# Routing attention and a bilinear feed-forward on one core: who sums the exponentials of the first batch element, and when weights are rounded

## The chip, the cores and the metric

The kernel runs on one core of a Trainium2 chip. The metric is device time in microseconds (us), and less is better. TensorE (PE) multiplies matrices into PSUM, VectorE (DVE), ScalarE (ACT) and GpSimd (POOL) work element by element, and SyncE (SP) issues most of the transfers. Each engine takes its instructions in the order in which the program gives them.

## What is computed

The input has 4 batch elements, 8 heads, 768 rows and a head dimension of 64. Queries and keys are assigned to one of 16 centroids per head, and a query sees only the keys of its own centroid. The attention output of each row (8 heads by 64) is the input of a feed-forward that multiplies two projections with each other.

```python
q_assign = np.argmax(np.einsum('bhsd,hcd->bhsc', q_n, c_n), axis=-1)
k_assign = np.argmax(np.einsum('bhsd,hcd->bhsc', k_n, c_n), axis=-1)
mask = q_assign[:, :, :, None] == k_assign[:, :, None, :]
scores = np.where(mask, scale * np.matmul(q, k.transpose(0, 1, 3, 2)), -1e9)
attn = np.exp(scores - np.max(scores, axis=-1, keepdims=True))
attn = attn / (np.sum(attn, axis=-1, keepdims=True) + 1e-09)
x = np.matmul(attn, v)            # then (B, H, S, D) -> (B*S, H*D)
out = (x @ w_a) * (x @ w_b) @ w_out    # w_a, w_b: 512 x 1536, w_out: 1536 x 512
```

The weights come as 64-bit numbers and are rounded to 32 bits on the chip.

## The kernel before

**The units.** Two heads form a pair, and there are 16 pairs, four (HP) to a batch element. The 768 query columns of a pair are two halves of 384 (HB), and its keys are six tiles of 128 (NJ). A unit u is one pair p, one half hf and one key tile j. The main loop (L580) runs over groups g of two units, six groups to a pair; l is g mod 6, so a half ends after l = 2 and after l = 5. The four pairs of the first batch element are the groups 0 to 23.

**A group.** `score` (L403) multiplies keys with queries for both units, the masking product of the one-hots first, and ScalarE exponentiates into a tile pt, of which there are four. For the two units of the group before, `add_up` (L431) adds each pt into acc, and `weigh` (L448) multiplies with the values into O. In the first batch element a half has ten additions of 128 x 384: two of them, for the second head at j = 1 and j = 3, are GpSimd's, and eight are VectorE's. In the later batch elements GpSimd has seven of ten. Then comes a preparation step of the next pair (`prep_steps`, L376): transposes at l = 0, similarity to the centroids at l = 1, the choice of a centroid by five VectorE instructions at l = 2 (`prep_assign`, L339), and at l = 4 both transposes of the one-hots (`prep_onehot`, L358).

**Denominators.** When a half has been summed, `denominators` (L465) multiplies acc with ones on TensorE, so that each column's sum stands in all rows, and ScalarE copies it to den. This happens at l = 4 and at l = 1, one group after the last addition was issued. `normalize` (L478) takes the reciprocal in three VectorE instructions at the end of a group (l = 5 and l = 3) and multiplies xT by it on GpSimd. `check_inverses` (L488) then reads den on ScalarE in the next group, right behind the two exponentials.

**The weights.** There are 36 parts of 128 x 512, 24 of w_a and w_b in three thirds of their columns, then 12 of w_out. `round_w` (L243) costs VectorE four instructions, ScalarE one (`size`) and GpSimd one addition, and `flush_w` (L270) ends it with a fifth VectorE instruction, issued in the next group or ahead of the next part. `size` has one buffer, so that ScalarE's `size` of a part waits for the flush of the part before. `due` (L564) says in which group each part is rounded. Behind each part `load_w` issues the transfer of the part after the next on SyncE's queue.

**The feed-forward.** When all four pairs of a half have been normalised, `ffn_ready` (L542) queues the pieces of that block. A piece is one projection of 128 output columns, and a group takes as many pieces as its share of columns (`PER_GROUP`) allows, about three. For the first batch element the first eight pieces use the first third of w_a and w_b alone. All of `ps_m`, the PSUM pool of the transposes, the denominators and the pieces, has three buffers.

**Names.** `ps_s` is the PSUM pool of the scores (two buffers), `ps_m` that of the rest (three), `ptp` the pool of pt (four), `wtp` that of the rounding's scratch tiles.

Of the kernel before, what the change touches and what calls it, by code (L numbers as in the profile page):

```python
# [30 lines left out]
P = 128  # L31
# [3 lines left out]
@with_exitstack  # L35
def kernel(
    ctx: ExitStack,
    tc: tile.TileContext,
    q: bass.AP,
    k: bass.AP,  # L40
    v: bass.AP,
    centroids: bass.AP,
    moe_w_a: bass.AP,
    moe_w_b: bass.AP,
    moe_w_out: bass.AP,
    out: bass.AP,
):
    nc = tc.nc

    B, H, S, D = q.shape  # L50
    NC = centroids.shape[1]
    DM, DF = moe_w_a.shape
    NJ = S // P
    HP = H // 2
    NCH = DM // P
    NF = DF // P
    assert D == 64 and NC == 16 and NJ == 6 and DM == H * D and H * NC == P

    const = ctx.enter_context(tc.tile_pool(name="const", bufs=1))
    ctx.enter_context(tc.manual_schedule())  # L60


    csb = const.tile([P, D], FP32)
    nc.scalar.dma_start(out=csb, in_=centroids.rearrange("h c d -> (h c) d"))
    c = {
        "wa_sb": const.tile([P, NCH, DF], FP32, name="wa_sb"),
        "wb_sb": const.tile([P, NCH, DF], FP32, name="wb_sb"),
        "wo_sb": const.tile([P, NF, DM], FP32, name="wo_sb"),
    }

    one = const.tile([P, 1], FP32)
    nc.vector.memset(one, 1.0)
    ce = const.tile([P, 1], FP32)
    ident = c["ident"] = const.tile([P, P], FP32, name="ident")
    masks.make_identity(nc, ident)
    identb = c["identb"] = const.tile([P, P], BF16, name="identb")
    ones = c["ones"] = const.tile([P, D], FP32, name="ones")
    nc.vector.memset(ones, 1.0)

    rank_i = const.tile([P, NC], INT32)  # L80
    nc.gpsimd.iota(rank_i, pattern=[[-1, NC]], base=NC, channel_multiplier=0)
    rank = c["rank"] = const.tile([P, NC], FP32, name="rank")

    cn = const.tile([P, 2, D], FP32)

    def centroids_in():

        nc.scalar.activation(out=ce, in_=one, func=AF.Sqrt)
        csq = const.tile([P, D], FP32)
        cs2 = const.tile([P, 1], FP32)  # L90
        nc.vector.tensor_tensor(out=csq, in0=csb, in1=csb, op=ALU.mult)
        nc.vector.tensor_reduce(out=cs2, in_=csq, axis=AX.X, op=ALU.add)
        cn0 = const.tile([P, 1], FP32)
        nc.scalar.activation(out=cn0, in_=cs2, func=AF.Sqrt)

        nc.scalar.activation(out=ce, in_=cn0, func=AF.Exp)

        cnm = const.tile([P, 1], FP32)
        nc.vector.tensor_scalar(out=cnm, in0=cn0, scalar1=1e-30, scalar2=None,
                                op0=ALU.max)  # L100
        cnr = const.tile([P, 1], FP32)
        nc.vector.reciprocal(out=cnr, in_=cnm)
        cnt = const.tile([P, 1], FP32)
        nc.vector.scalar_tensor_tensor(out=cnt, in0=cs2, scalar=cnr[:, 0:1],
                                       in1=cn0, op0=ALU.mult, op1=ALU.add)
        cne = const.tile([P, 1], FP32)
        nc.vector.tensor_scalar(out=cne, in0=cnt, scalar1=0.5, scalar2=1e-6,
                                op0=ALU.mult, op1=ALU.add)
        crinv = const.tile([P, 1], FP32)
        nc.vector.reciprocal(out=crinv, in_=cne)  # L110
        for a in range(2):
            nc.vector.tensor_scalar(out=cn[:, a, :], in0=csb,
                                    scalar1=crinv[:, 0:1], scalar2=None,
                                    op0=ALU.mult)
        nc.vector.tensor_copy(out=rank, in_=rank_i)
        nc.vector.tensor_copy(out=identb, in_=ident)

    cT = c["cT"] = const.tile([P, P], FP32, name="cT")  # L120
    cTb = c["cTb"] = const.tile([P, HP, 2 * NC], FP32, name="cTb")
    nc.gpsimd.memset(cTb, 0.0)

    n_far = const.tile([1, 1], INT32, name="n_far")
    with ExitStack() as fast:
        short_path(nc, tc, fast, c, cn, centroids_in, n_far, q, k, v, moe_w_a, moe_w_b,
                   moe_w_out, out)

    redo = nc.values_load(n_far[0:1, 0:1], min_val=0, max_val=P,
                          skip_runtime_bounds_check_because="a count of rows")  # L130
    with tc.If(redo > 0):
        with ExitStack() as slow:
            long_path(nc, tc, slow, c, q, k, v, out)


def short_path(nc, tc, ctx, c, cn, centroids_in, n_far, q, k, v, moe_w_a,
               moe_w_b, moe_w_out, out):


    B, H, S, D = q.shape  # L140
# [23 lines left out]
    xtp = pool("xtp", 2)  # L164
    hp_ = pool("hp", 2)
    hap = pool("hap", 2)
    yp = pool("yp", 1)
    rawp = pool("rawp", 2)
    wtp = pool("wtp", 1)
    ps_s = pool("ps_s", 2, PS)  # L170
    ps_m = pool("ps_m", 3, PS)
    ps_o = pool("ps_o", 1, PS)
# [70 lines left out]
    def round_w(i):  # L243
        flush_w()
        w = w_parts[i][0]
        wi = w.bitcast(INT32)
        raw = raws.pop(i)
        halves = lambda dt: raw.bitcast(dt).rearrange("p (n two) -> p n two", two=2)
        lo, hi = halves(UINT32)[:, :, 0], halves(INT32)[:, :, 1]


        nc.vector.tensor_scalar(out=wi, in0=hi, scalar1=3, scalar2=0x3FFFFFF8,
                                op0=ALU.logical_shift_left,
                                op1=ALU.bitwise_and)
        nc.vector.scalar_tensor_tensor(out=wi, in0=hi, scalar=SIGN_TOP, in1=wi,
                                       op0=ALU.bitwise_and, op1=ALU.bitwise_or)

        rest = wtp.tile([P, WN], FP32, name="rest")
        nc.vector.tensor_scalar(out=rest.bitcast(INT32), in0=wi,
                                scalar1=SIGN_EXP, scalar2=None,  # L260
                                op0=ALU.bitwise_and)
        nc.vector.scalar_tensor_tensor(out=rest, in0=lo, scalar=2.0 ** -52,  # L262
                                       in1=rest, op0=ALU.mult, op1=ALU.mult)

        size = wtp.tile([P, WN], FP32, name="size")
        nc.scalar.activation(out=size, in_=halves(FP32)[:, :, 1], func=AF.Abs)  # L266
        nc.gpsimd.tensor_tensor(out=w, in0=w, in1=rest, op=ALU.add)
        flush.append((w, size))
# [107 lines left out]
    def prep_steps(p):  # L376
# [3 lines left out]
        def both(*fs):  # L380
# [4 lines left out]
            both(lambda: prep_sim(p), lambda: load_v(p)),  # L385
            lambda: prep_assign(prep_across(p)),
            lambda: None,
            both(lambda: prep_onehot(p, 0), lambda: prep_onehot(p, 1)),
            lambda: None,
        ]  # L390

# [38 lines left out]

    def add_up(u):  # L431
        p, hf, j = where(u)
        if j == 0:
            return
        if j == 1:
            accs[p, hf] = accp.tile([P, 2, HB], FP32, name="acc")
        acc = accs[p, hf]
        for a in range(2):
            if p < HP:
                eng = nc.gpsimd if a == 1 and j in (1, 3) else nc.vector  # L440
            else:
                eng = nc.gpsimd if a == 1 or j in (2, 4) else nc.vector
            eng.tensor_tensor(  # L443
                out=acc[:, a, :],
                in0=probs[u - 1][:, a, :] if j == 1 else acc[:, a, :],
                in1=probs[u][:, a, :], op=ALU.add)
# [17 lines left out]

    def denominators(p, hf):  # L465

        ps = ps_m.tile([P, 512], FP32, name="m")
        acc = accs.pop((p, hf))
        for a in range(2):
            nc.tensor.matmul(out=ps[a * D:(a + 1) * D, 0:HB], lhsT=ones,  # L470
                             rhs=acc[:, a, :], start=True, stop=True)
        den = denp.tile([P, HB], FP32, name="den")
        n = 4 * p + 2 * hf
        nc.scalar.activation(out=den, in_=ps[:, 0:HB], func=AF.Copy,  # L474
# [22 lines left out]
    def ffn_block(b, blk):  # L497
# [25 lines left out]
        def down(n):  # L523
            ps = ps_m.tile([P, 512], FP32, name="m")
            for f in range(NF):
                nc.tensor.matmul(out=ps, lhsT=box["h"][:, f, n * P:(n + 1) * P],  # L526
                                 rhs=wo_sb[:, f, :],
                                 start=(f == 0), stop=(f == NF - 1))
            y = yp.tile([P, DM], FP32, name="y")
            nc.scalar.copy(out=y, in_=ps)  # L530
            rows = out[b * S:(b + 1) * S, :].rearrange(
                "(p j) n -> p j n", j=NJ)[:, 3 * blk + n, :]
# [24 lines left out]
    GPP = UPP // 2  # L557
    NG = NPAIR * GPP
    PER_GROUP = (2 * NF * NCH * HB + 3 * NF * DM) * 2 // (HP * GPP)
    credit = 0  # L560

    due = {g: [i] for i, g in enumerate((1, 4, 6, 7, 10, 13, 16, 19))}  # L564
    for i in range(8, len(w_parts)):
        due.setdefault(20 + int((i - 8) / 1.5), []).append(i)

    prep_transpose(0, 0)
    centroids_across()
    prep_transpose(0, 1)  # L570
    prep_transpose(0, 2)
    load_v(0)
    load_w(0)
    load_w(1)
# [5 lines left out]
    for g in range(NG + 3):  # L580
# [13 lines left out]
            weigh(before)  # L594
        if g < NG:
            ready[l]()
        if g % 3 == 1 and 3 < g:
            denominators(*divmod(g // 3 - 1, 2))
        parts = due.get(g, [])

# [17 lines left out]
        if l == 0 and p + 1 < NPAIR:  # L618
            prep_transpose(p + 1, 2)
            load(p + 2)  # L620
        if l == 5 or l == 3 and 6 < g < NG or g == NG + 2:
            ph = (p, 0) if l == 5 else (p - 1, 1)
            normalize(*ph)
            if ph[0] % HP == HP - 1:
                ffn_ready(ph[0] // HP, ph[1])
# [248 lines left out]
```

## Time and profile before

| | us |
|---|---|
| median of 3 runs | 1214.0 (1213.69 to 1214.56) |
| the profiled execution | 1212.46 |
| its span, first to last instruction | 1210.6 |
| TensorE busy in it | 1154.6 (95%) |
| VectorE, ScalarE, GpSimd busy | 408.1, 333.2, 276.6 |

The page divides the span into 40 equal slices. TensorE's busy digits are 6987597999 in the first ten slices and 9 in nearly all later ones; VectorE's are 5999967566 in the first ten. A busy digit of TensorE says that matmuls were in flight, not that they ran at the full clock: the row PEclk gives the granted clock beside it.

### The profile page before, as it was taken

Reading aid. Unit: us, or ns where it says so; the run is one execution under the profiler, and the core shown is the slowest. Engines: PE = TensorE matmul, PEld = TensorE weight load, DVE = VectorE, ACT = ScalarE, POOL = GpSimd, SP = SyncE. Lnnn points to the kernel's source line nnn. Section 1 sums busy time; section 2 is a strip of 40 time slices with the busy share of each in tenths; the row PEclk is TensorE's granted clock in tenths of the full one; section 3 lists DMA queues with packets and bytes.
Section 4 is the critical chain, followed back from the end, with each engine's and each line's share of the span. In section 5 each row is a group of like instructions: output and inputs, shape, how many; then the busy total and the mean of one; then the engine's idle time right before and its main releaser. Section 6 shows DMA issues by size and latency. Waiting matters only on the chain.

```text
span 1210.6 us, 11842 instructions
## 1 busy us (share of the span) xinstructions
PE 1154.6 (95%) x4723; PEld 578.0 (48%) x4723; DVE 408.1 (34%) x614; ACT 333.2 (28%) x608; POOL 276.6 (23%) x261
## 2 busy tenths in 40 slices
PE   6987597999999999999999999999999999999998
PEld 3433253555554445554455544555445544554553
DVE  5999967566621211222022221222111220200100
ACT  4654333323323222322322222321322211100000
POOL 2333324334413221222221132121211321000000
PEclk9999798999999999999999999999999999999999
DMA  5323332321202001010200101010000000000000
GB/s 155 94 75 84 95 92 87 88 74 53 74 1 57 18 22 35 1 40 9 57 1 1 39 18 48 1 40 1 18 22 1 1 9 18 1 1 26 1 1 28
DMA packets 60782, 44.91 MB, mean 37 GB/s; under 512 B 48432, under 2 KB 53040, under 8 KB 60720
## 3 DMA queue, kind: packets, MB, share of 16 engines
q1 hardware_dynamic: 59744, 42.21, 12.1%
q10 hardware_dynamic: 976, 1.87, 0.4%
q8 instruction: 39, 0.64, 0.2%
q14 instruction: 23, 0.19, 0.1%
HBM read 37.78 MB, written 6.29 MB: 36 GB/s over the span
## 4 chain that ended last, share of the span: by engine, by line
PE 86%; DVE 8%; issue 2%; POOL 2%; ACT 2%; DMA 0%; DVEq 0%; POOLq 0%; ACTq 0%
PE m L505 42%; PE m L526 21%; PE O L454 8%; PE s L420 8%; DVE den L483 3%; PE s L411 3%; PE m L307 2%; PE m L470 1%; DVE acc L443 1%; PE m L323 1%; POOL xT L485 1%; DVE wa_sb L274 1%; DVE rest L262 1%; PE m L334 1%; DVE wb_sb L274 0%
## 5 line engine op out<-in xcount | busy, mean ns | idle before, releaser
L505 PE MATMUL m<-xT,wa_sb 128*128 128x384 f32 x768 | 268.6, 493 | 16.7 <-ACT ohT L374 13.4
L505 PE MATMUL m<-xT,wb_sb 128*128 128x384 f32 x768 | 268.3, 493 | 0.0
L526 PE MATMUL m<-wo_sb,h 128*128 128x512 f32 x576 | 251.2, 594 | 0.0
L520 DVE TENSOR_TENSOR h<-ha,m 128x384 f32<-128x384 f32 x96 | 53.1, 554 | 536.2 <-PE m L505 536.1
L443 POOL TENSOR_TENSOR acc<-acc,pt 128x384 f32<-128x384 f32 x152 | 155.4, 1035 | 241.6 <-ACT pt L427 233.9
L505 PEld LDWEIGHTS m<-xT,wa_sb 128*128 128x128 f32 x768 | 145.1, 192 | 120.6 <-ACT ohT L374 18.0
L505 PEld LDWEIGHTS m<-xT,wb_sb 128*128 128x128 f32 x768 | 145.4, 192 | 111.3 <-ACT pt L427 10.2
L427 ACT ACTIVATE pt<-s 128x768 f32<-128x768 f32 x192 | 145.7, 809 | 124.8 <-PE s L420 89.0
L526 PEld LDWEIGHTS m<-wo_sb,h 128*128 128x128 f32 x576 | 108.7, 191 | 133.9 <-issue 129.7
L454 PE MATMUL O<-pt,v 128*64 128x384 f32 x768 | 145.0, 499 | 0.7 <-ACT xT L462 0.7
L420 PE MATMUL s<-qkT 64*128 64x384 f32 x768 | 144.4, 496 | 0.0
L516 ACT COPY ha<-m 128x384 f32<-128x384 f32 x96 | 45.9, 478 | 351.5 <-PE m L505 351.5
L443 DVE TENSOR_TENSOR acc<-acc,pt 128x384 f32<-128x384 f32 x104 | 87.1, 868 | 140.0 <-POOL acc L443 140.0
L485 POOL TENSOR_TENSOR xT<-xT,den 128x384 f32<-128x384 f32 x32 | 34.8, 1088 | 344.7 <-DVE den L483 343.1
L454 PEld LDWEIGHTS O<-pt,v 128*64 128x64 f32 x768 | 46.8, 136 | 88.5 <-issue 84.8
L420 PEld LDWEIGHTS s<-qkT 64*128 64x128 f32 x768 | 73.2, 193 | 32.1 <-issue 2.4
L530 ACT COPY y<-m 128x512 f32<-128x512 f32 x24 | 14.0, 585 | 255.4 <-PE m L526 195.6
L483 DVE RECIPROCAL den<-den 128x128 f32<-128x128 f32 x96 | 82.2, 912 | 5.5 <-ACT den L474 5.5
L411 PE MATMUL s<-ohT 64*128 64x384 bf16 x384 | 50.3, 334 | 22.9 <-ACT pt L427 22.2
L411 PEld LDWEIGHTS <-ohT 64*128 64x128 bf16 x384 | 12.2, 94 | 73.3 <-issue 63.0
L443 POOL TENSOR_TENSOR acc<-pt 128x384 f32<-128x384 f32 x32 | 37.7, 1179 | 36.5 <-ACT pt L427 36.5
L266 ACT ACTIVATE size<-raw 128x512 f32<-128x512 f32 x36 | 24.6, 685 | 51.2 <-DVE wa_sb L274 19.7
(82 smaller groups left out, 516.1 us busy)
## 6 DMA issues: line engine op xcount, KB each, us to landing
raw<-in_moe_w_out_dram SPq DMA_DIRECT2D x12, 512.0 KB, 3.2
out_dram<-y SPq DMA_DIRECT2D x24, 256.0 KB, 2.0
qk<-in_q_dram SPq DMA_DIRECT2D x30, 192.0 KB, 3.9
qk<-in_k_dram SPq DMA_DIRECT2D x30, 192.0 KB, 4.2
v<-in_v_dram SPq DMA_DIRECT2D x15, 384.0 KB, 4.6
raw<-in_moe_w_a_dram SPq DMA_DIRECT2D x11, 512.0 KB, 3.5
raw<-in_moe_w_b_dram SPq DMA_DIRECT2D x11, 512.0 KB, 3.5
raw<-in_moe_w_a_dram ACTq DMA_DIRECT2D x1, 512.0 KB, 4.5
```

Source lines behind the costliest of these rows:

```text
L266: nc.scalar.activation(out=size, in_=halves(FP32)[:, :, 1], func=AF.Abs)
L411: nc.tensor.matmul(out=s[:, a, 0:HB], lhsT=ohTs[p][r, S + j * P:S + (j + 1) * P], rhs=ohTs[p][r, hf * HB:(hf + 1) * HB], start=True, stop= ...
L420: nc.tensor.matmul(out=s[:, a, 0:HB], lhsT=qkTs[p][r, S + j * P:S + (j + 1) * P], rhs=qkTs[p][r, hf * HB:(hf + 1) * HB], start=False, stop ...
L427: nc.scalar.activation(out=pt, in_=s[:, :, 0:HB], func=AF.Exp, scale=SCALE)
L443: eng.tensor_tensor(out=acc[:, a, :], in0=probs[u - 1][:, a, :] if j == 1 else acc[:, a, :], in1=probs[u][:, a, :], op=ALU.add)
L454: nc.tensor.matmul(out=O_of[0][a * D:(a + 1) * D, 0:HB], lhsT=vs[p][:, a, j, :], rhs=probs[u][:, a, :], start=(j == 0), stop=(j == NJ - 1))
L483: nc.vector.reciprocal(out=part, in_=part)
L485: nc.gpsimd.tensor_tensor(out=x, in0=x, in1=den, op=ALU.mult)
L505: nc.tensor.matmul(out=ps[:, 0:HB], lhsT=w_sb[:, ch, f * P:(f + 1) * P], rhs=xTs[b][:, ch, t0:t0 + HB], start=(ch == 0), stop=(ch == NCH - 1))
L516: nc.scalar.copy(out=box["a"], in_=ps[:, 0:HB])
L520: nc.vector.tensor_tensor(out=box["h"][:, f, :], in0=box["a"], in1=ps[:, 0:HB], op=ALU.mult)
L526: nc.tensor.matmul(out=ps, lhsT=box["h"][:, f, n * P:(n + 1) * P], rhs=wo_sb[:, f, :], start=(f == 0), stop=(f == NF - 1))
```

## The change

It touches five things.

1. In the first batch element the last key tile of a half (j = 5) is no longer added on VectorE. `denominators` multiplies its pt with ones as well, into the same PSUM sums, with two more matmuls.
2. The remaining additions of the first batch element, eight per half, are all on VectorE; GpSimd has none of them there.
3. `denominators` runs one group earlier in the first batch element (l = 3 and l = 0, in the group in which the last addition is issued), and `normalize` at the end of l = 4 and l = 1.
4. Parts are rounded at g = 0, 3, 6, ... 21, so that eight parts, a third of w_a and w_b, precede group 23 (before, 14 parts were due by the end of group 23); the other 28 follow from group 23, 1.75 a group instead of 1.5 from group 20. `size` gets two buffers, and the output tile y takes the buffer of `rest`.
5. `prep_onehot` of the queries moves from the preparation step of l = 4 to the end of that group, and two small casts of the start are issued later.

```diff
+    def casts():
+        nc.vector.tensor_copy(out=rank, in_=rank_i)
+        nc.vector.tensor_copy(out=identb, in_=ident)
...
-    yp = pool("yp", 1)
+    sizep = pool("sizep", 2)
...
-        size = wtp.tile([P, WN], FP32, name="size")
+        size = sizep.tile([P, WN], FP32, name="size")
...
-            both(lambda: prep_onehot(p, 0), lambda: prep_onehot(p, 1)),
+            lambda: prep_onehot(p, 1),
...
-        if j == 0:
+        if j == 0 or j == NJ - 1 and p < HP:
             return
...
-            if p < HP:
-                eng = nc.gpsimd if a == 1 and j in (1, 3) else nc.vector
-            else:
-                eng = nc.gpsimd if a == 1 or j in (2, 4) else nc.vector
+            many = p >= HP and (a == 1 or j in (2, 4))
+            eng = nc.gpsimd if many else nc.vector
...
-        acc = accs.pop((p, hf))
-        for a in range(2):
-            nc.tensor.matmul(out=ps[a * D:(a + 1) * D, 0:HB], lhsT=ones,
-                             rhs=acc[:, a, :], start=True, stop=True)
+        terms = [accs.pop((p, hf))]
+        if p < HP:
+            terms.append(probs[p * UPP + hf * NJ + NJ - 1])
+        for n, t in enumerate(terms):
+            for a in range(2):
+                nc.tensor.matmul(out=ps[a * D:(a + 1) * D, 0:HB], lhsT=ones,
+                                 rhs=t[:, a, :], start=(n == 0),
+                                 stop=(n == len(terms) - 1))
...
-            y = yp.tile([P, DM], FP32, name="y")
+            y = wtp.tile([P, DM], FP32, name="rest")
...
+    EARLY = HP * GPP + 1
...
-    due = {g: [i] for i, g in enumerate((1, 4, 6, 7, 10, 13, 16, 19))}
+    due = {3 * i: [i] for i in range(8)}
     for i in range(8, len(w_parts)):
-        due.setdefault(20 + int((i - 8) / 1.5), []).append(i)
+        due.setdefault(23 + int((i - 8) / 1.75), []).append(i)
...
+    casts()
...
-        if g % 3 == 1 and 3 < g:
+        late = int(g > EARLY)
+        if g % 3 == late and 0 < g - late:
             denominators(*divmod(g // 3 - 1, 2))
...
-        if l == 5 or l == 3 and 6 < g < NG or g == NG + 2:
-            ph = (p, 0) if l == 5 else (p - 1, 1)
+        if l == 4 and p + 1 < NPAIR:
+            prep_onehot(p + 1, 0)
+        if g <= EARLY:
+            first, second = 4, 1
+        else:
+            first, second = 5, 3 if g < NG else 2
+        ph = {first: (p, 0), second: (p - 1, 1)}.get(l)
+        if ph in den_of:
             normalize(*ph)
```

## Rows read from the trace of the kernel before

**Rows 1.** Six stretches: length; busy PE, PEld, DVE, ACT, POOL; clock; DMA; GB/s.

```profile
17.10:40.35 23.25, 23.22 (x152) 10.77 (x153) 18.13 (x27) 14.81 (x23) 7.10 (x6) 0.94 0.36 89
40.35:66.90 26.55, 25.24 (x165) 11.30 (x163) 25.05 (x36) 12.77 (x23) 8.29 (x8) 1.00 0.36 102
66.90:96.85 29.95, 25.99 (x165) 11.70 (x164) 29.50 (x41) 18.78 (x36) 10.97 (x9) 0.94 0.28 75
96.85:131.90 35.05, 25.90 (x163) 11.59 (x163) 33.13 (x49) 15.63 (x29) 12.19 (x10) 0.90 0.38 109
131.90:209.36 77.46, 58.57 (x233) 29.35 (x232) 56.93 (x84) 26.81 (x50) 31.34 (x27) 0.85 0.31 90
209.36:340.00 130.64, 129.58 (x555) 68.86 (x554) 78.97 (x116) 43.67 (x79) 46.48 (x42) 1.00 0.22 67
```

**Rows 2.** TensorE's waits from 17 to 132 us: total, times, longest.

```profile
PE s L411 <- ACT pt L427: 13.6, 8, 6.4
```

**Rows 3.** The same view from 132 to 210 us.

```profile
PE s L411 <- ACT pt L427: 8.6, 4, 7.6
PE m L505 <- ACT ohT L374: 7.0, 1, 7.0
PE m L505 <- POOL xT L485: 3.3, 1, 3.3
```

**Rows 4.** Timeline around group 22: start, length, what, idle before and releaser.

```profile
120.15 0.69 DVE L274 SCALAR_TENSOR_TENSOR wa_sb<-size,wa_sb 128x512 f32<-128x512 f32 x1 [1.37 <-POOL wa_sb L267]
...
120.88 0.68 ACT L266 ACTIVATE size<-raw 128x512 f32<-128x512 f32 x1 [6.48 <-DVE wa_sb L274]
...
122.30 0.51 PE L411 MATMUL s<-ohT 64*128 64x384 bf16 x2 [6.41 <-ACT pt L427]
```

**Rows 5.** Timeline, VectorE: a rounding, the reciprocals behind it, its flush.

```profile
126.56 0.41 DVE L252 TENSOR_SCALAR wa_sb<-raw 128x512 int32<-128x512 int32 x1
...
128.81 2.57 DVE L483 RECIPROCAL den<-den 128x128 f32<-128x128 f32 x3
...
131.71 1.48 DVE L274 SCALAR_TENSOR_TENSOR wa_sb<-size,wa_sb 128x512 f32<-128x512 f32 x1
```

**Rows 6.** Groups by line, 17 to 132 us: count, busy us, mean ns, idle.

```profile
L443 DVE TENSOR_TENSOR acc<-acc,pt 128x384 f32<-128x384 f32 x49 | 37.3, 818 | 0.0
L262 DVE SCALAR_TENSOR_TENSOR rest<-raw,rest 128x512 f32<-128x512 uint32 x11 | 7.7, 699 | 0.4
...
L443 POOL TENSOR_TENSOR acc<-pt 128x384 f32<-128x384 f32 x7 | 8.4, 1196 | 22.3 <-ACT pt L427 22.3
```

**Rows 7.** Timeline: additions without and with GpSimd at work beside them.

```profile
88.72 1.96 DVE L443 TENSOR_TENSOR acc<-acc,pt 128x384 f32<-128x384 f32 x4
...
97.21 2.56 DVE L443 TENSOR_TENSOR acc<-acc,pt 128x384 f32<-128x384 f32 x3
97.38 1.51 POOL L267 TENSOR_TENSOR wa_sb<-wa_sb,rest 128x512 f32<-128x512 f32 x1 [1.81 <-DVE rest L262]
```

**Rows 8.** Timeline, groups 3 and 4: TensorE's starts, VectorE's choice and additions.

```profile
29.29 0.50 PE L411 MATMUL s<-ohT 64*128 64x384 bf16 x4
29.39 0.56 DVE L343 TENSOR_REDUCE mx<-m 128x24 f32<-128x384 f32 x1 [0.67 <-PE m L334]
...
32.23 2.76 DVE L443 TENSOR_TENSOR acc<-acc,pt 128x384 f32<-128x384 f32 x4
32.45 0.50 PE L411 MATMUL s<-ohT 64*128 64x384 bf16 x4
```

**Rows 9.** Timeline, TensorE: one half's denominators, one group's products with the values.

```profile
36.38 0.87 PE L470 MATMUL m<-acc,ones 128*64 128x384 f32 x4
...
38.90 1.51 PE L454 MATMUL O<-pt,v 128*64 128x384 f32 x8
```

**Rows 10.** The chain that ended last: start, length, what (three pieces).

```profile
165.06 7.94 PE m L505 x24
```

**Rows 11.** TensorE's waits from 280 us to the end.

```profile
PE m L505 <- ACT ohT L374: 5.3, 5, 1.1
```

More of the change, by code (lines that the diff above doesn't have):

```diff
@@ L114, in centroids_in @@
                                     op0=ALU.mult)
-        nc.vector.tensor_copy(out=rank, in_=rank_i)
-        nc.vector.tensor_copy(out=identb, in_=ident)
     cT = c["cT"] = const.tile([P, P], FP32, name="cT")
@@ L125 @@
     with ExitStack() as fast:
-        short_path(nc, tc, fast, c, cn, centroids_in, n_far, q, k, v, moe_w_a, moe_w_b,
-                   moe_w_out, out)
+        short_path(nc, tc, fast, c, cn, centroids_in, casts, n_far, q, k, v,
+                   moe_w_a, moe_w_b, moe_w_out, out)
     redo = nc.values_load(n_far[0:1, 0:1], min_val=0, max_val=P,
@@ L133, with short_path @@
             long_path(nc, tc, slow, c, q, k, v, out)
-def short_path(nc, tc, ctx, c, cn, centroids_in, n_far, q, k, v, moe_w_a,
-               moe_w_b, moe_w_out, out):
+def short_path(nc, tc, ctx, c, cn, centroids_in, casts, n_far, q, k, v,
+               moe_w_a, moe_w_b, moe_w_out, out):
     B, H, S, D = q.shape
```

## The prediction

> **What bounds the kernel now.** I read the page's busy slices first: TensorE is the engine that matters, and it has holes only early. Then I cut the span where groups begin and read the busy times of each stretch [rows 1]. The first four rows are the four pairs of the first batch element. The first pair is TensorE's own speed: busy 23.22 of 23.25 us. The next three have the same work and take 26.55, 29.95 and 35.05, while VectorE's busy time climbs to 33.13 of 35.05. So from the second pair on VectorE sets the pace. The fifth row, five groups with the first feed-forward pieces, is worse: TensorE is busy 58.57 of 77.46 and its mean clock is 0.85. In the sixth row TensorE is busy 129.58 of 130.64, and from there it bounds the kernel to the end.
>
> The waits say how VectorE reaches TensorE. Up to 132 us TensorE waits 13.6 us for exponentials [rows 2], behind that 8.6 for the same, 7.0 for a copy of the one-hots and 3.3 for a normalised xT [rows 3]. The exponentials were not slow. Where two parts are rounded in one group, ScalarE stands 6.48 us at `size`, whose single buffer the flush on VectorE has not released, the exponentials of the next group are queued behind it, and TensorE stands 6.41 [rows 4].
>
> **How much there is to win.** A pair has two denominators, and the first row holds one, so a pair without stalls is 23.25 + 0.87 [rows 9] = 24.1 us. Four pairs would be 23.25 + 3 x 24.1 = 95.6; they took 131.90 - 17.10 = 114.8. Loss A: 19.2. The fifth stretch holds five groups at 24.1 / 6 = 4.0 and eleven pieces (3, 3, 2, 0 and 3 by the code's shares) at 7.94 / 3 = 2.65 [rows 10]: 20.1 + 29.1 = 49.2 of 77.46. Loss B: 28.3, of which 18.9 is idle and the rest the lower clock. Loss C: five waits of 1.06 us for the one-hots' copy, 5.3 [rows 11], and 1.06 in the sixth stretch: 6.4. Together 53.9. The last microseconds and the start stay out.
>
> **Part 1 and 2, the sums.** TensorE gets two more 128 x 64 matmuls per half (four records). Eight such records take 1.51 and four 0.87 [rows 9], so four more cost 0.64 to 0.76; I take 0.75, times eight halves 6.0 us, all on the path. The dearer end is 4 x 7.94 / 24 = 1.3 a half, 10.6, if the two heads' matmuls did not overlap as they do in these rows. VectorE still has eight additions a half: it loses two and takes over GpSimd's two. What it gains is quiet. Four additions take 1.96 alone, 0.49 each; three take 2.56 with a GpSimd addition beside them, and the mean is 0.818 [rows 6, 7]. A flush takes 0.69 alone and 1.48 beside GpSimd [rows 4, 5], so a GpSimd addition costs VectorE about 0.79. Two groups of seven GpSimd additions ran up to 132 us (1.196 us each in the one shown) [rows 6], so 14 x 0.79 = 11.1 us of VectorE goes away; the ends are 14 x 0.33 = 4.6 (one addition at the difference of the means) and 14 x 1.196 = 16.7.
>
> The Trainium skill's page "SBUF — State Buffer", section "Who interferes with whom", says that a VectorE instruction with two SBUF inputs and a GpSimd instruction that reads SBUF exclude each other for the whole instruction. By that the upper end, 16.7, would hold, and the time below would come out some 2 us shorter, as an estimate; the trace shows 1.1 us lost beside a GpSimd instruction of 1.51 [rows 7], less than that.
>
> **Part 4, the roundings.** One costs VectorE 2.25 us up to the next instruction and 0.69 to 1.48 for its flush [rows 4, 5]: 3.7 as it ran. Up to 132 us eleven ran [rows 6] of the fourteen due; eight will by the end of group 22: 3 x 3.7 = 11.1 less. VectorE's budget for the four pairs is then 105.8 (its busy times in the first four rows) - 11.1 - 11.1 + 6.0 (seven additions and a set of reciprocals that ran late, 7 x 0.49 + 2.57 [rows 5, 7]) = 89.6 us, against 95.6 + 6.0 = 101.6 for TensorE. VectorE stops being the bound there, but it is 88% loaded. The parts go to groups 23 to 28, which have eleven roundings, as many as the fifth stretch had (eight due and the three late ones), but TensorE there has 18 pieces instead of 11, so 5 x 4.0 + 4.0 + 18 x 2.65 = 72 us for six groups, against 56.93 + 7 x 0.55 (an estimate for a piece's product, like one addition beside a PSUM tile) = 61 of VectorE. The second buffer of `size` takes away the wait of rows 4 outright: ScalarE no longer stands for a flush of the part just before. SyncE's `load_w` moves with the parts, ahead of the q and k loads at l = 0; these have a whole pair to land, and I cost that at nothing. If that cover were gone, a late load would hold the transposes of the next pair by the length of a rounding, about 3 us a pair.
>
> **Part 3, the new wait.** TensorE now reaches the denominators in the group that issues the last additions (j = 4). At l = 3 these stand on VectorE behind the choice of centroids, 29.39 to 32.23 [rows 8], and take 2 x 0.49, so they end some 3.8 us after TensorE began the group; TensorE gets there 3.16 us after it (the distance of two group starts without preparation [rows 8]). That is 0.7 us a pair if VectorE is on time, and more by whatever it lags. Queued behind the denominators on TensorE are the next scores, and behind these the exponentials. At l = 0 the transposes lie ahead and cover it. I take 7 us of stalls for A in all (from 3, four times 0.7, to 15, two a half).
>
> Normalising a group or two earlier starts the first pieces in group 23 instead of 24 and the rest in 26 instead of 28, which fills TensorE where it stood. The first piece of the second block still needs the last reciprocals and a GpSimd product, some 3.8 us behind their issue; one group of scores covers most of it. I take 6 us of stalls for B (2 to 16).
>
> **Part 5.** With the queries' one-hots behind the pieces, only the keys' and the denominators' buffers of `ps_m` are held while ScalarE waits in `check_inverses`, and a piece finds the third. That should take all of C (6.4; between none and all of it). The casts are two small copies which VectorE now does while it waits for the similarities; costed at nothing, at most two additions' length, 1.0 us, if that wait were gone.
>
> **The sum.** 53.9 - 6.0 = 47.9 us at best; less 7 (A) and 6 (B): 34.9. Against the profiled execution, 1212.46 (1.9 more than its span), that is 1177.6, and the median of the runs is 1.5 above this execution: 1179.
>
> **The rivals.** *One stage keeps its loss.* For: VectorE is 88% loaded in the pairs and as a rule late, and if GpSimd's additions cost it only 4.6, its budget is 96 of 101.6; the parts of the second third are rounded one group before they are used. Against: both budgets leave room. If A keeps 18 of its 19, the time is 1190; if B keeps 20 of 28, 1193; with the dearer matmuls up to 1200.
> *Slower: the denominators wait for VectorE's lag.* The wait removed at `size` would come back as a wait for acc, at eight halves, with all of TensorE's work queued behind. It decides from 47.9 / 8 = 6.0 us a half: from there nothing is won. The longest waits of TensorE that VectorE causes now are 6.4 and 7.6 [rows 2, 3]; at 7.6 a half the time is 1214 - 47.9 + 61 = 1227. Against it: a lag of this size came from two roundings in one group, and now none has two before group 23.
> *The change does nothing.* VectorE has as many additions as before and 28 roundings crowd the start of the feed-forward: the loss moves from A to B, within 2 us of 1214.
>
> **How the numbers follow.** Forecast (1167 to 1187): 0.67. One stage keeps its loss (1187 to 1200): 0.24. Nothing: 0.04. Slower: 0.05. The range takes the first two, 1167 to 1200; its ends are the sum with least stalls (47.9 less 1) and that of the first rival. A measurement of this kernel can tell 0.2%, about 2.4 us, from no change; so faster 0.91, same 0.04, slower 0.05.
>
> **What would show it.** Right: groups 0 to 23 about 12 us shorter; no wait of ScalarE's `size` for a flush; the clock at 1.00 in nearly all of 17 to 200 us; the five later waits gone; additions near 0.5 us before the feed-forward. Wrong: TensorE waiting at the denominators for acc by more than 2 us a half, pieces waiting for w_a or w_b, or VectorE still busy over 95% in the second to fourth pair.

## The result and the profile after

The changed kernel takes 1171.4 us (median; 1170.0 to 1172.4) against 1213.9 for the kernel before: a ratio of 0.965, 95% interval 0.9633 to 0.9667, or 42.5 us less. The forecast was 1179, with a range of 1167 to 1200. The spans of the two profiled executions are 1210.6 and 1170.0 us, 40.6 us apart; what is read from traces below adds up to this figure.

All of it lies in the first 210 us and at the later transposes of the one-hots. The first fence shows the stretches of the changed kernel in the columns of [rows 1]: length; busy PE, PEld, DVE, ACT, POOL with instructions; clock; DMA share; GB/s. The first line is most of the first pair. The next three, 26 us each, are nearly pairs 2 to 4: the scores of groups 6, 12 and 18 begin at 43.64, 70.07 and 96.50, so a pair takes 26.4 us.

```profile
17.00:40.00 23.00, 21.95 (x136) 10.56 (x135) 14.96 (x27) 12.68 (x20) 2.79 (x2) 0.88 0.38 98
40.00:66.00 26.00, 25.61 (x169) 11.38 (x166) 24.09 (x37) 16.83 (x30) 5.28 (x4) 1.00 0.32 79
66.00:92.00 26.00, 25.61 (x171) 11.69 (x171) 24.08 (x37) 16.72 (x30) 5.27 (x4) 1.00 0.33 87
92.00:118.00 26.00, 25.61 (x171) 11.49 (x169) 24.09 (x38) 16.40 (x31) 5.10 (x4) 1.00 0.30 84
118.00:145.00 27.00, 27.00 (x130) 14.46 (x128) 19.98 (x33) 11.54 (x22) 7.17 (x7) 1.00 0.30 87
145.00:210.00 65.00, 64.58 (x283) 33.84 (x279) 48.10 (x71) 25.02 (x44) 27.24 (x25) 1.00 0.33 96
```

TensorE is busy 25.61 of every 26 us in the pairs and nearly all of the time behind them, with a granted clock of 1.00 from 40 us on, where [rows 1] had 25.24 of 26.55, 25.99 of 29.95, 25.90 of 35.05 and 58.57 of 77.46. VectorE is still busy 24.1 of 26 in the pairs.

The second fence is the list of all of TensorE's waits in the changed kernel (who waited for whom, total us, times, longest us). It answers [rows 2, 3 and 11].

```profile
PE m L309 <- DVE nfar L281: 6.7, 1, 6.7
PE m L366 <- DVE oh L356: 3.2, 1, 3.2
PE m L474 <- DVE acc L443: 1.6, 4, 0.4
PE m L510 <- ACT ohT L371: 0.9, 1, 0.9
PE s L413 <- DVE ohT L374: 0.7, 1, 0.7
PE m L336 <- ACT sim L330: 0.6, 1, 0.6
PE m L510 <- DVE sim L347: 0.4, 1, 0.4
```

The first two and the two of 0.7 and 0.6 belong to the start. What is left of the rest is 2.9 us: the new wait at the denominators (L474), 0.4 us once a pair, and two small ones. Waits for the exponentials are no longer in the list.

Three starts on TensorE, from its timeline, give the split: group 23, its first feed-forward piece, and group 29.

```profile
119.76 0.50 PE L413 MATMUL s<-ohT 64*128 64x384 bf16 x4
...
122.92 2.85 PE L510 MATMUL m<-xT,wa_sb 128*128 128x384 f32 x8
...
192.55 0.50 PE L413 MATMUL s<-ohT 64*128 64x384 bf16 x4
```

The groups 0 to 23 without pieces end at 122.9 instead of 131.9: 9.0 us. They begin at 18.4 instead of 17.1, so they are 10.3 us shorter. Group 29 starts at 192.55 with 18 pieces done, instead of 209.36 with 11. Seven pieces at 2.65 [rows 10] are 18.6, so TensorE is 16.8 + 18.6 = 35.4 us ahead there, 26.4 of it won in groups 24 to 28. The other 5.2 of the 40.6 us come later, in the place of the waits of [rows 11]: behind 280 us TensorE has no wait left.

### The profile page after: what moved, and what is told of

It is laid out like the page before. It is cut to its first block, busy times and chain, and to the rows that moved or that the text cites. A ratio compares the mean times of both kernels' runs of the same rounds, so it can differ in the third digit from the quotient of the medians.

```text
span 1170.0 us, 11898 instructions
## 1 busy us (share of the span) xinstructions
PE 1151.0 (98%) x4755; PEld 576.3 (49%) x4755; DVE 396.3 (34%) x614; ACT 335.9 (29%) x608; POOL 256.1 (22%) x245
## 4 chain that ended last, share of the span: by engine, by line
PE 94%; DVE 4%; issue 1%; POOL 1%; DMA 0%; ACT 0%; DVEq 0%; POOLq 0%; ACTq 0%
PE m L510 41%; PE m L531 21%; PE O L454 11%; PE s L422 10%; PE s L413 3%; PE m L474 3%; PE m L309 2%; PE m L325 1%; PE m L366 1%; PE m L336 1%; DVE den L488 0%; DVE acc L443 0%; DVE sim L347 0%; DVE mx L345 0%; POOL wo_sb L269 0%
## 5 line engine op out<-in xcount | busy, mean ns | idle before, releaser
L510 PE MATMUL m<-xT,wa_sb 128*128 128x384 f32 x768 | 265.0, 488 | 1.3 <-ACT ohT L371 0.9
L510 PE MATMUL m<-xT,wb_sb 128*128 128x384 f32 x768 | 265.6, 489 | 0.0
L443 POOL TENSOR_TENSOR acc<-acc,pt 128x384 f32<-128x384 f32 x144 | 146.8, 1033 | 266.9 <-ACT pt L429 263.2
L422 PE MATMUL s<-qkT 64*128 64x384 f32 x768 | 140.8, 486 | 0.0
L443 DVE TENSOR_TENSOR acc<-acc,pt 128x384 f32<-128x384 f32 x96 | 76.7, 828 | 158.9 <-POOL acc L443 158.5
L535 ACT COPY rest<-m 128x512 f32<-128x512 f32 x24 | 14.1, 585 | 250.3 <-PE m L531 250.3
L443 DVE TENSOR_TENSOR acc<-pt 128x384 f32<-128x384 f32 x40 | 30.2, 772 | 51.7 <-ACT pt L429 51.7
L443 POOL TENSOR_TENSOR acc<-pt 128x384 f32<-128x384 f32 x24 | 27.2, 1134 | 45.7 <-ACT pt L429 45.7
L309 PE MATMUL m<-ident,qk 128*128 128x128 f32 x192 | 28.5, 289 | 6.7 <-DVE nfar L281 6.7
```

Source lines behind the costliest of these rows:

```text
L309: nc.tensor.transpose(out=ps[:, n * P:(n + 1) * P], in_=qks[p][:, w, j].rearrange("p a d -> p (a d)"), identity=ident)
L422: nc.tensor.matmul(out=s[:, a, 0:HB], lhsT=qkTs[p][r, S + j * P:S + (j + 1) * P], rhs=qkTs[p][r, hf * HB:(hf + 1) * HB], start=False, stop ...
L443: eng.tensor_tensor(out=acc[:, a, :], in0=probs[u - 1][:, a, :] if j == 1 else acc[:, a, :], in1=probs[u][:, a, :], op=ALU.add)
L510: nc.tensor.matmul(out=ps[:, 0:HB], lhsT=w_sb[:, ch, f * P:(f + 1) * P], rhs=xTs[b][:, ch, t0:t0 + HB], start=(ch == 0), stop=(ch == NCH - 1))
```

## The experiments

Each kernel is given with its ratio to the kernel before, measured beside it, since the base moved by 2 us between series (1212.3 to 1214.3). Microseconds are differences of these ratios times 1213.85. An interval is 0.001 to 0.0025 wide to either side, in most kernels 0.0017, or 2 us, so that two kernels can be told apart from about 3 us on.

### Undoing the second buffer of size, and doing it alone

```diff
-    sizep = pool("sizep", 2)
+    sizep = pool("sizep", 1)
```

> The changed kernel (1171.4 us) with one buffer for size again. If ScalarE's wait for the flush of the part before was a cause of the holes by itself, that wait comes back in the groups that round two parts (23, 24, 25, 27 and 28 among them), with the exponentials queued behind it: 8 to 25 us slower, 1180 to 1196. If the holes came from VectorE's load, which stays relieved here, ScalarE's wait is covered: within 3 us of 1171.

0.9658 (0.9642 to 0.9674): 1.0 us, within the intervals nothing. The waits of ScalarE in its trace, from 17 to 340 us, show that the stall itself did come back:

```profile
ACT size L268 <- DVE wo_sb L276: 18.4, 5, 7.7
...
ACT size L268 <- DVE wb_sb L276: 8.4, 4, 3.1
...
ACT size L268 <- DVE wa_sb L276: 6.8, 3, 2.9
```

These are 33.6 us of waiting at size, up to 7.7 at a time, and yet TensorE's list of waits is the changed kernel's, line for line but for the start. The second buffer alone in the kernel before (with y sharing the buffer of rest, to make room):

> The kernel before (1212.3 to 1214 us) with two buffers for size alone (the output tile shares the buffer of rest, as in the change, to make room). The run with one buffer in the changed kernel cost nothing. If ScalarE's wait was only a sign of VectorE being late, the exponentials gain little, since they wait for the same VectorE through pt: 0 to 5 us faster, at 1208 or above. If the wait is a cause where VectorE is late: 8 to 20 us faster, 1193 to 1205.

0.9994 (0.9985 to 1.0004): nothing. Its trace shows where the wait goes. From 17 to 340 us ScalarE's waits at size for a flush fall from 47.5 us to 1.6. In the fourth pair it stands 5.3 us at size all the same, until 122.23. It had to read a part there whose transfer was issued at 118.64, when VectorE had read the part before out of the buffer, and such transfers land 3.5 us behind their issue; that it waited for this transfer is inferred, since the profile names a VectorE instruction that ended just then. TensorE's waits for the exponentials fall from the 22.2 us of [rows 2, 3] to 13.2, and waits for acc, which the kernel before did not have, appear:

```profile
PE s L411 <- ACT pt L427: 13.2, 10, 5.4
...
PE m L470 <- DVE acc L443: 6.0, 2, 5.0
```

In group 22 TensorE now stands 4.98 us at the denominators instead of 6.41 at the scores. So the wait of [rows 4] was a sign and not a cause. ScalarE stood for a flush because VectorE was late, and with a second buffer both engines wait for the same late VectorE elsewhere.

### The rounding schedule

```diff
-    due = {3 * i: [i] for i in range(8)}
+    due = {g: [i] for i, g in enumerate((1, 4, 6, 7, 10, 13, 16, 19))}
     for i in range(8, len(w_parts)):
-        due.setdefault(23 + int((i - 8) / 1.75), []).append(i)
+        due.setdefault(20 + int((i - 8) / 1.5), []).append(i)
```

> The changed kernel with the rounding schedule of before: 14 parts instead of 10 due by the end of group 23, two in each of the groups 20 and 22, while size keeps its two buffers. If VectorE's load bounds the fourth pair, its busy time there, about 23 of 26 us now, grows by some five roundings of 3.0 us and the pair by about 10: 1179 to 1187. If only the wait at size mattered, within 3 us of 1171.

0.9787 (0.9762 to 0.9812): 16.6 us lost, about what the theory of VectorE's load gave (the median, 1188.6, is just above its range). The trace says more than load. In its timeline around group 21, VectorE rounds the two parts of group 20 between the choice of centroids and the last additions, and TensorE stands at the denominators:

```profile
116.40 0.42 DVE L254 TENSOR_SCALAR wa_sb<-raw 128x512 int32<-128x512 int32 x1
120.72 0.42 DVE L254 TENSOR_SCALAR wb_sb<-raw 128x512 int32<-128x512 int32 x1
122.97 2.09 DVE L443 TENSOR_TENSOR acc<-acc,pt 128x384 f32<-128x384 f32 x2
123.57 2.44 PE L474 MATMUL m<-acc,ones 128*64 128x384 f32 x3 [6.88 <-DVE acc L443]
```

The new schedule in the kernel before, alone:

> The kernel before with the rounding schedule of the change alone, size with one buffer, sums and denominators as before. Undoing the schedule in the changed kernel cost 17 us. If the parts add up, it is 15 to 20 us faster than before, 1194 to 1199. If the schedule is worth something only with the other relief of VectorE, 5 to 10 us faster; if one buffer of size chokes groups that round two parts, nothing.

0.9904 (0.9888 to 0.9921): 11.7 us won, less than the 16.6 of undoing it, and between the two ranges expected. TensorE's waits for the exponentials halve, to 10.7 us from the 22.2 of [rows 2, 3]. The waits for the one-hots' copies stay: 17.4 us, and 13.4 in the kernel before [rows 3, 11]. These copies are ScalarE's, which waits 33.6 us in `check_inverses` for GpSimd's xT up to 340 us (30.5 in the kernel before). TensorE's waits:

```profile
PE m L505 <- ACT ohT L374: 17.4, 7, 8.9
PE s L411 <- ACT pt L427: 10.7, 6, 3.3
```

### The sums

The additions of before go back into the changed kernel: two of ten a half on GpSimd, the last tile's on VectorE, no extra matmuls.

```diff
-        if j == 0 or j == NJ - 1 and p < HP:
+        if j == 0:
...
-            many = p >= HP and (a == 1 or j in (2, 4))
-            eng = nc.gpsimd if many else nc.vector
+            if p < HP:
+                eng = nc.gpsimd if a == 1 and j in (1, 3) else nc.vector
+            else:
+                eng = nc.gpsimd if a == 1 or j in (2, 4) else nc.vector
...
-        if p < HP:
-            terms.append(probs[p * UPP + hf * NJ + NJ - 1])
```

> The changed kernel with the additions of before: two of ten a half on GpSimd, the last tile's on VectorE, no extra matmuls; all else stays, the earlier denominators too. TensorE saves 8 x 0.75 = 6 us. If VectorE is still near its limit in the pairs, four GpSimd additions a pair cost it about 4 x 0.79 = 3.2 us, and the last additions now lie in front of the denominators, one more us a half: 3 to 12 us lost, so between 1168 and 1178. If VectorE has room to spare, the time falls to 1166.

0.9688 (0.9671 to 0.9704): 4.6 us lost. Then all ten on VectorE, without the matmuls:

```diff
-        if j == 0 or j == NJ - 1 and p < HP:
+        if j == 0:
...
-        if p < HP:
-            terms.append(probs[p * UPP + hf * NJ + NJ - 1])
```

> The changed kernel with all ten additions of a half on VectorE and no extra matmuls. TensorE saves 6 us. With the two additions back on GpSimd and the last on VectorE it was 3 us slower. If that loss is the last additions lying in front of the denominators, it stays: two more additions of 0.5 us a half, 1.0 us of wait at eight halves, 1171 to 1176. If it was the contention with GpSimd, the 6 us are won: 1165 to 1168.

0.965 (0.9634 to 0.9666): the time of the changed kernel. TensorE has 6 us less to do and waits longer. Its waits for acc are 6.9 us in both kernels, against 1.6. Sums on VectorE alone:

```profile
PE m L472 <- DVE acc L443: 6.9, 4, 1.9
```

and with GpSimd's two:

```profile
PE m L474 <- DVE acc L445: 6.9, 4, 2.1
```

So the last tile on TensorE pays for itself and no more, and what is won lies in taking GpSimd out, 4.6 us with an interval that reaches from about 2 to 7 (the medians, 1174.6 and 1171.5, lie 3.2 apart). How it wins that is not what was forecast. The groups of VectorE from 40 to 118 us (count, busy us, mean ns, idle before), changed kernel first:

```profile
L443 DVE TENSOR_TENSOR acc<-acc,pt 128x384 f32<-128x384 f32 x36 | 22.0, 671 | 0.0
...
L443 DVE TENSOR_TENSOR acc<-pt 128x384 f32<-128x384 f32 x12 | 12.6, 1091 | 0.0
L276 DVE SCALAR_TENSOR_TENSOR wa_sb<-size,wa_sb 128x512 f32<-128x512 f32 x3 | 2.1, 693 | 1.3 <-ACT size L268 1.3
L276 DVE SCALAR_TENSOR_TENSOR wb_sb<-size,wb_sb 128x512 f32<-128x512 f32 x2 | 1.4, 678 | 0.0
```

With GpSimd's additions:

```profile
L445 DVE TENSOR_TENSOR acc<-acc,pt 128x384 f32<-128x384 f32 x42 | 26.9, 697 | 0.3
...
L276 DVE SCALAR_TENSOR_TENSOR wa_sb<-size,wa_sb 128x512 f32<-128x512 f32 x3 | 4.4, 1475 | 3.5 <-POOL wa_sb L269 3.5
L276 DVE SCALAR_TENSOR_TENSOR wb_sb<-size,wb_sb 128x512 f32<-128x512 f32 x3 | 4.4, 1471 | 3.5 <-POOL wb_sb L269 3.5
...
L445 DVE TENSOR_TENSOR acc<-pt 128x384 f32<-128x384 f32 x5 | 2.8, 551 | 0.0
```

Additions and flushes together are 22.0 + 12.6 + 2.1 + 1.4 = 38.1 us in the one (48 additions, 5 flushes) and 26.9 + 2.8 + 4.4 + 4.4 = 38.5 in the other (47 and 6). VectorE did not get quieter: the slow pieces moved. Without GpSimd's additions a half's first two run beside the rounding's own GpSimd addition and take 1.09 each on the mean (one 0.55, the other 1.63) instead of 0.55; the flush then takes 0.69 instead of 1.48. What did fall is VectorE's idle time ahead of the flushes: from 7.0 us, all of it for GpSimd, to 1.3, for ScalarE's size.

### The place of normalize, and the early pieces

```diff
-        if g <= EARLY:
-            first, second = 4, 1
+        if g <= EARLY + 1:
+            first, second = 5, 2
```

> The changed kernel with normalize one group later in the first batch element (end of l = 5 and l = 2 instead of 4 and 1); the pieces start in group 24 and the second block in group 27. If the early pieces fill holes, group 23 is short of TensorE work while it rounds two parts on VectorE: 3 to 8 us slower, 1174 to 1179. If TensorE is simply full, the same work in another order: within 2 us of 1171.

0.9785 (0.9768 to 0.9801): 16.4 us lost, more than either theory gave. It moves two things, the three reciprocals and the start of the feed-forward. The next kernel moves the second alone: `normalize` stays and `ffn_ready` is called where it was called before the change (end of groups 23 and 27).

```diff
+    later = {}
...
-                ffn_ready(ph[0] // HP, ph[1])
+                later[g + {22: 1, 25: 2}.get(g, 0)] = (ph[0] // HP, ph[1])
+        if g in later:
+            ffn_ready(*later.pop(g))
```

> The changed kernel with its normalize where it is (end of l = 4 and l = 1), but the feed-forward's blocks queued where the kernel before queued them (pieces from group 24, the second block from group 28). Moving both one group later cost 17 us. If that was the place of the three reciprocals, 2.6 us of VectorE in front of the last additions and so of the denominators, this costs little: within 4 us of 1171. If it was the missing pieces, it costs as much: 1183 to 1190.

0.9776 (0.9759 to 0.9792): 15.3 us lost with the reciprocals in their new place. So the loss does not come from the place of the reciprocals alone: the missing early pieces by themselves cost nearly as much as both. Why, its timeline shows. Group 23 rounds two parts on VectorE, and without pieces TensorE passes through it in 3.2 us:

```profile
123.80 0.41 DVE L254 TENSOR_SCALAR wa_sb<-raw 128x512 int32<-128x512 int32 x1
128.11 0.42 DVE L254 TENSOR_SCALAR wb_sb<-raw 128x512 int32<-128x512 int32 x1
130.36 2.09 DVE L443 TENSOR_TENSOR acc<-acc,pt 128x384 f32<-128x384 f32 x2
130.97 2.44 PE L474 MATMUL m<-acc,ones 128*64 128x384 f32 x3 [4.22 <-DVE acc L443]
...
190.09 5.49 PE L510 MATMUL m<-xT,wb_sb 128*128 128x384 f32 x8 [4.84 <-DVE h L525]
```

In the changed kernel VectorE does the same roundings in the same place, and its last additions are no earlier. But TensorE has three pieces to do in group 23 and needs the sum at 135.04:

```profile
128.54 0.42 DVE L254 TENSOR_SCALAR wb_sb<-raw 128x512 int32<-128x512 int32 x1
...
131.26 1.85 DVE L443 TENSOR_TENSOR acc<-acc,pt 128x384 f32<-128x384 f32 x2
...
135.04 0.87 PE L474 MATMUL m<-acc,ones 128*64 128x384 f32 x4
```

The kernel with the later start has the same work to do. It loses by these two stands, 4.22 and 4.84 us, by 1.3 at the next denominators (together 10.4 of the 14.9 us between the two spans), and by the half clock behind the stands (a matmul of these denominators with acc takes 0.85 to 0.90 us, in the changed kernel 0.49 to 0.54). The reciprocals' place does show in the pairs: one group later, TensorE's waits for acc were 11.2 us, 2.8 at the longest, against 7.0 in all with the late pieces, of which 5.5 are the stands above. In time the two moves together cost only 1.1 us more than the late pieces alone, which is within the intervals, and no kernel here moves the reciprocals alone.

The earlier denominators and normalize in the kernel before, and with them the earlier pieces, without the rest (the edits of the change in the loop, ten additions and the old schedule):

> The kernel before with the earlier denominators and normalize alone (ten additions as before, 14 parts by group 23, one-hots together). Undoing the place of normalize cost 17 us of 42. If the place is good by itself: 10 to 20 us faster, 1193 to 1203. If it needs the lighter schedule, because with 14 parts TensorE waits at the earlier denominators for late additions (up to 6.9 us where the schedule alone was undone): within 4 us of 1213, or slower.

0.9843 (0.9827 to 0.9859): 19.1 us won, at the upper end of what the theory of a gain by itself gave. The rival's mechanism is there too and is only outweighed: TensorE waits 17.3 us for acc, 8.9 at once.

```profile
PE m L470 <- DVE acc L443: 17.3, 4, 8.9
...
PE m L505 <- POOL xT L485: 4.8, 1, 4.8
```

### The one-hots together

```diff
-            lambda: prep_onehot(p, 1),
+            both(lambda: prep_onehot(p, 0), lambda: prep_onehot(p, 1)),
...
-        if l == 4 and p + 1 < NPAIR:
-            prep_onehot(p + 1, 0)
```

> The changed kernel with both transposes of the one-hots in one step again. If their PSUM buffers held up the pieces, the later waits of 1.06 us at six groups come back: 4 to 7 us slower, 1175 to 1178. If another part removed these waits (it has no place in the later batch elements), within 2 us of 1171.

0.9716 (0.9696 to 0.9736): 8.0 us lost (5.8 by the medians, 1177.3 against 1171.4). The waits of [rows 11] are back, with one of 3.2 us among them:

```profile
PE m L510 <- ACT ohT L376: 7.4, 5, 3.2
```

### Moving the choice behind the last additions

```diff
-            lambda: prep_assign(prep_across(p)),
             lambda: None,
+            lambda: prep_assign(prep_across(p)),
```

> The changed kernel with the choice of centroids (transposes and five VectorE instructions, 2.9 us) at l = 3, behind the last additions instead of ahead of them. If the additions behind the choice are what TensorE still waits for at the denominators, its four waits of 0.4 us go and the clock does not change: 1 to 4 us faster, 1167 to 1170. If the choice is then late for the one-hots at l = 4, a wait there takes its place: 1171 or more.

0.9644 (0.9628 to 0.966): 0.7 us, nothing that can be told. Its waits for acc are 1.4 us in place of 1.6, so the choice was not what the denominators waited for; a wait of 1.0 for xT came in. With all ten additions on VectorE besides:

> All ten additions on VectorE, no extra matmuls, and the choice at l = 3. All ten alone gave the time of the changed kernel, 1171.5: 6 us of TensorE against 6.9 us of waits for acc. If these waits come from the choice lying ahead, they go and the 6 us are won: 1164 to 1167. If VectorE, busy 25.6 of 26 us in a pair, is then the bound, nothing is won over the changed kernel: 1169 to 1172.

0.9662 (0.9646 to 0.9678): nothing is won over the changed kernel, as its second theory has it. Waits for acc of 4.6 us stay and waits for exponentials return (2.0 in six); VectorE is busy 25.2 of 26 us in a pair, so that TensorE can't use what it saved. No version here beats the changed kernel.

## Why the prediction was right, and where its steps were not

**Right.** TensorE was the engine to read, and its holes were the thing to price: 53.9 us of loss less 6.0 of new matmuls gave a ceiling of 47.9, and 40.6 came between the two profiled spans. By stages the forecast was 19.2 - 6.0 - 7 = 6.2 for the pairs, 28.3 - 6 = 22.3 behind them and 6.4 for the one-hots. Measured are 10.3, of which a later start takes 1.3 back; 26.4; and 5.2 for the one-hots (6 to 8 by their own run). The stalls, put at 7 and 6, are thus 2.9 and 1.9, the low ends of their ranges, and that is why the time lies below the forecast. The new matmuls take 0.74 us a half in the trace (135.74 to 136.48), as they were put. The new wait at the denominators was put at 0.7 us a pair at l = 3 and is 0.4. The earlier pieces do fill TensorE: groups 23 to 28 take 72.8 us, and 72 was forecast. The clock is 1.00 from 40 us on, though 0.88 in the 23 us before.

Two lines of the prediction do not follow from its sum. The sign "groups 0 to 23 about 12 us shorter" leaves out the 6.0 us of matmuls; the sum has 6.2. The lower end of the range takes 1 us of stalls, where the least that it names are 3 and 2, which give 1171.

**Wrong in mechanism: size.** The prediction said that the second buffer "takes away the wait of rows 4 outright" and told from these rows how the wait reaches TensorE. The wait for the flush goes, and nothing is won, in either kernel. The profile's releaser named the last event, VectorE's flush; I took the engine standing in between as the cause. One sentence of the slower rival had it right: the wait removed at size "would come back as a wait for acc". In the kernel before it did, by 6.0 us.

**Wrong in size and kind: the quiet on VectorE.** The step 14 x 0.79 = 11.1 us took the loss beside GpSimd as a price that goes away with each GpSimd addition. The loss moved to other instructions, and the busy time of additions and flushes did not fall (38.1 against 38.5). The sign "additions near 0.5 us" did not come true: they take 0.67 and 1.09 on the mean. The rule of the Trainium skill, page "SBUF — State Buffer", section "Who interferes with whom", names who excludes whom, and the trace agrees with it: of the two additions beside the rounding's GpSimd addition one takes 1.63 us instead of 0.55. The 16.7 us that I worked out from it were as wrong as my 11.1, since both assumed that VectorE had nothing else to meet; how a time 2 us shorter follows from them is not worked out. The prediction also set the 1.1 us that VectorE lost against GpSimd's 1.51 and found it less than the rule has it. But the rounding's GpSimd addition takes 1.27 us where VectorE stands still beside it (at 126.20 and 135.38 us in the kernel with the late pieces), so that the 1.51 holds a loss of GpSimd's own.

**Right in part by luck: the budget.** Over groups 0 to 23 VectorE's budget came out: it is busy 91.5 of the 104.5 us from 18.4 to 122.9, 88%, where 89.6 of 101.6 were forecast. But with GpSimd's additions put back it is busy 90.0 us in these groups, so the 11.1 us of quiet did not bring it there; what did, beside the roundings that moved away, was not taken apart. In pairs 2 to 4 it is busy 24.1 of 26 us, 93%, close to the 95% that was named a sign of being wrong, and TensorE waits 0.4 us a pair. The undone schedule and the late pieces show that the sum of VectorE's work is not what decides. From 17 to 145 us VectorE is busy 106.3 and 110.6 us in them, and 107.2 in the changed kernel. They put two roundings, 6.6 us from the first instruction to the additions behind them, ahead of the last additions of a half in a group where TensorE has nothing else to do. That is the mechanism of the rival that ended on the other side, "the denominators wait for VectorE's lag": 6.9 us at once where the schedule was undone and 8.9 where the earlier timing stood alone, once each and not at eight halves, so it stayed below its point of decision of 6.0 a half.

**What the parts are worth.** Undone one at a time: schedule 16.6, pieces 15.3 (with the reciprocals 16.4), one-hots 8.0, sums 4.6, size 1.0: 45.5 in all against 42.5. Done alone: timing 19.1, schedule 11.7, size 0.7. I had not priced the early pieces apart; they turned out the equal of the schedule, and the two belong together: pieces start in the group in which the double roundings start. No kernel here takes out both at once, so the nearness of the sums, 45.5 and 42.5, says little of how they combine.

**Open.** Where the 4.6 us of GpSimd's additions go, when the waits for acc are 6.9 us with and without them, is settled only in part. Groups 0 to 23 take 107.7 us with them and 105.5 without. The difference lies in the second pair, 28.8 us against 26.6: with them the denominators' matmuls behind a stand of 2.11 us took 0.85 to 0.90 us each, half the clock, and without them, behind a stand of 1.86, 0.49 to 0.54. The mean clock from 40 to 66 us agrees with it (0.93 with them, 1.00 without). The rest of the 4.6 is not in these two executions, whose spans differ by 1.5. The two casts that moved were not tried alone. The first scores begin at 18.4 us in the changed kernel and at 17.1 before it, but at 16.9 to 18.6 in the ten kernels with the casts moved and at 16.8 to 18.0 in the four without, one execution each, so what the casts cost can't be told.

## What to carry to other kernels

Where engines run in order, look at what is queued ahead of the one instruction that the bounding engine needs, not at the sum of the feeding engine's work: a long piece of side work belongs in a group in which the bounding engine has other work to do. A wait that the profile shows on an engine in between may be a sign of a late third engine; give it a second buffer alone before believing it a cause. Two engines that slow each other do not stop when one gives up some of its instructions, if the other then runs beside the rest.

## What the runs showed of the hardware that was not expected

The loss beside GpSimd goes by the GpSimd instruction and not by the number of VectorE's. Three additions beside a GpSimd addition of 1.51 us lost 1.1 us [rows 7], two additions beside one of 1.52 us the same 1.1 (2.10 in place of 0.98), and a flush beside one of GpSimd's shorter instructions (128 x 384) 0.79. One VectorE instruction bears it: of the two additions one took 0.55 us and the other 1.63. It can't be taken away by moving some of GpSimd's instructions, if VectorE then meets the others. And a stand of TensorE can cost twice: behind a stand of 4.22 us the next matmuls of the same kind took 0.85 to 0.90 us instead of 0.49 to 0.54, half the clock (1.2 GHz in place of 2.4; 0.94 granted on the mean of 118 to 145 us); behind stands of 0.4 us, in the changed kernel, they kept 0.49 to 0.54.
